# Batch 0's mirrored rows loaded in natural order, their pairs turned and added by TensorE

## The chip, the cores and the metric

The kernel runs on one core of one Trainium2 chip. The metric is the time of one execution on the device in microseconds, as the median of several runs. The profiled execution is one more run, taken with the hardware profiler.

## The reference, cut to what matters

```python
def _attn_ref(x):                      # x: (8, 3136, 256) float32
    X = np.fft.fft(x, axis=1)
    X = np.fft.fft(X, axis=2)
    return X.real.astype(np.float32)

def _moe_ref(x, w_in, conv_w, w_out):  # w_in (256, 1024), conv_w (3, 1024), w_out (1024, 256)
    h = np.maximum(x @ w_in, 0.0)
    # depthwise convolution of width 3 along the sequence, zeros outside
    conv_out = sum(conv_w[k] * shifted(h, k - 1) for k in range(3))
    gate = 1.0 / (1.0 + np.exp(-conv_out))
    return (h * gate @ w_out).astype(np.float32)

out = _moe_ref(_attn_ref(x), w_in, conv_w, w_out)
```

The real part of a two-dimensional Fourier transform, then a gated feed-forward block. The weights come as float64, x as float32.

## The kernel before

The transform of a real input is symmetric, so the kernel works with half of the output rows (NK = S/2 + 1) and with sums and differences of input rows. For each batch it loads x in two halves (`load_ops`), adds to each row its mirror in the sequence and in the feature direction, takes sums and differences further (`fold_ops`), and multiplies the folded tiles with cosine and sine tables (`units`): odd and even output rows, cosine and sine parts, giving two tiles PQ[b]. The second transform and `w_in` are multiplied into one matrix G (`blocks`, `column`), so a step of the main loop does two matmuls (`products`), adds and subtracts them for a row and its mirror with a clamp at zero (`combine`), does the convolution and the gate, and multiplies with `w_out` (`mm2`). One step is one batch, one chunk of the sequence (CUTS) and one of eight blocks of 128 hidden features; loads, folds and units of the next batches are spread over the steps by a table of cycles (`at`, `side`).

All queues are in program order: what is written earlier for an engine runs earlier on it. Tiles come from pools with a fixed number of buffers, and a new tile in a pool waits until the oldest is no longer in use. The change acts in the prologue, before the first step. There:

- `load_ops(0, h)` loads half h of batch 0. A tile `xh` has 8 slots of two rows for each of 98 partitions (99 in the second half, whose last partition holds edge rows). Slots 0 to 3 come by a plain transfer from SP's queue (L119), slots 4 to 7, the mirrored rows, by four indirect transfers from GpSimd's queue (L132) with the index tile `idx`, which lists the partitions backwards.
- `fold_ops(0)` is the list of VectorE steps of both halves: `pair` (L157, L160) adds the mirrored slots to the plain ones, reading features backwards; `both` (L168) adds or subtracts two sums; `evens` (L172, L173); `feats` (L194, L195) folds along the features. `single` and the lines behind it (L179, L200, L202) write the edge columns on GpSimd. `scaled` (L218) turns an operand on ScalarE.
- `mirror_tables` (L319), `mirror_even` (L270) and `mend_row` (L312) complete the tables on ScalarE.
- `taps` turns the convolution weights with an identity on TensorE. `Weight.parts` narrows float64 to float32 (L654 to L677): on VectorE alone, or, where it is given `room`, with one step (L656) on ScalarE.
- `keep_on` issues matmuls of 128 x 128 by 128 x 512 whose result is not used.
- After the folds TensorE runs the four odd units in quarters (`part`), then the feature row (`feature`), `odd_first` (which adds odd entries of the last row to all partitions, from PQ), the even units and `even_first` (the same for even entries, from one row of `e`). Closing sums of the units are on VectorE (L401 to L434, L371 to L385).
- Then come `flip`, `store`, `spread`, the first `seed` and `products` (line L816 and the matmuls to pa and pb), the narrowing of `w_in[1]`, `copies` (L837) and the first `combine` (L845).

The lines of every matmul are those of the helper `mm` (L93), so matmuls are told apart by their tiles.

Of the kernel before, what the change touches and what calls it, by code (L numbers as in the profile page):

```python
# [37 lines left out]
def kernel(  # L38
# [56 lines left out]
    def spare():  # L95
# [8 lines left out]
    nc.gpsimd.iota(idx, pattern=[[0, 1]], base=2 * (NP - 1), channel_multiplier=-2,  # L104
                   allow_small_or_imprecise_dtypes=True)
    sg = const.tile([P, 2, 2], F32, name="sg")
    nc.gpsimd.memset(sg[:, 0], -1.0)
    nc.gpsimd.memset(sg[:, 1], 1.0)

    def load_ops(b, h, eng, other=None, held=False):  # L110


        def plain():
            t = xp.tile([P, 8, 2, D], F32, name="xh", tag="xh")
            xh[b, h] = t
            if held:

                nc.gpsimd.memset(t[0:1, 0, 0, 0:1], 0.0)
# [3 lines left out]

        def zero():
            t = xh[b, h]
            for s0, n, r in ((0, 4, 0), (4, 3, 1), (7, 1, 0)):
                (other or eng).dma_start(out=t[NP:KR, s0:s0 + n], in_=bass.AP(
                    tensor=x.tensor, offset=x.offset + (b * S + r * Q4) * D,
                    ap=[[D, 1], [Q4 * D, n], [0, 2], [1, D]]))
# [11 lines left out]
        return [plain] + [zero] * h + [mirrored(m) for m in range(4)]  # L140

    def fold_ops(b):
# [4 lines left out]
        def half(h):  # L147
# [18 lines left out]
            def both(to, op):  # L166
                def f():
                    vt(flat(to, to + 2), flat(0, 2), flat(2, 4), op=op)  # L168
                return f
# [14 lines left out]
            def feats(odd):  # L184
                def f():
# [12 lines left out]
                    single(odd)()  # L198
                    if odd:
                        gt(w[k, 2:4, qs, P - 1], t()[k, 7:5:-1, :, P], sg[k], op=ALU.mult)  # L200
                    else:
                        nc.gpsimd.tensor_copy(ea[b][k, :, qs], v[:, :, :, P])  # L202
# [28 lines left out]
            ops = [pair(0), pair(2), both(6, ALU.subtract), feats(1), both(4, ALU.add), turned, evens, feats(0)]  # L231
            return ops, {3: single(1), 7: single(0)}, {4: scaled}
# [8 lines left out]
    parted = {}  # L241
# [111 lines left out]
    def units(b):  # L353
# [83 lines left out]
        def feature():  # L437
# [11 lines left out]
            def copy(p):  # L449
                e = hp.tile([P, HW], F32, name="h", tag="h")  # L450
                a_["e"] = [e[:, i * (HO + 2):(i + 1) * (HO + 2)] for i in range(2)]
# [19 lines left out]
        def row():  # L471
            er[b] = erp.tile([1, NK], F32, name="er", tag="er")

        def odd_first(p, n):

            for i in range(2):
                mm(p[:, 1 + 2 * i:n:4], sel[:, i * P:(i + 1) * P], PQ[b][1][:, 1 + 2 * i:n:4], i == 0, True)
# [712 lines left out]
```

## Time and profile before

| | |
|---|---|
| median of 3 runs | 1162.02 us (1161.68 to 1164.53) |
| profiled execution | 1164.47 us, span 1162.7 us |
| mean granted TensorE clock | 0.996 |
| DMA | 167.49 MB, mean 144 GB/s |

A row of the timeline reads: start in us, duration in us, engine, line, operation, tile written <- tiles read, shape, number of instructions merged into the row, and in brackets the idle time of the engine before it with what ended it. PE is TensorE's matmul, PEld its weight load, DVE VectorE, ACT ScalarE, POOL GpSimd, SP the queue of SyncE; a q behind a name is the engine's issuing side. Where rows of one engine overlap, several instructions of other rows ran in between. The granted clock is the share of full speed that TensorE was given.

### The profile page before, as it was taken

How to read it: one execution, taken by the hardware profiler on the slowest of the kernel's cores; microseconds unless marked ns; L12 is line 12 of the kernel's file. 1: busy time of each engine (PE TensorE's matmuls, PEld its weight loads, DVE VectorE, ACT ScalarE, POOL GpSimd, SP SyncE). 2: the span in 40 equal slices, each digit the busy share in tenths (PEclk: the TensorE clock that was granted, in tenths of full speed). 3: DMA queues.
4: the chain of work that ended last, by engine and by line, in shares of the span. 5: the costliest groups of instructions: out<-in, count | busy, mean ns of one | idle time of the engine just before them, and what ended most of it. 6: DMA issues, size and time to landing. Idle time of an engine off the chain costs nothing.

```text
span 1162.7 us, 15082 instructions
## 1 busy us (share of the span) xinstructions
PE 1141.6 (98%) x4834; PEld 893.5 (77%) x4834; DVE 959.8 (83%) x1449; ACT 900.7 (77%) x1702; POOL 379.4 (33%) x493
## 2 busy tenths in 40 slices
PE   6999999999999999999999999999999999999998
PEld 4767777787778777877777877777778787777777
DVE  8699889988987989888878879788886767777775
ACT  3588877877777878887877777887877778888885
POOL 7335523633243152415233332422121221122223
PEclk9899999999999999999999999999999999999999
DMA  9777986786757586757675766865665556666664
GB/s 251 147 122 170 163 153 143 171 174 148 156 121 177 123 186 137 179 108 165 140 175 124 151 139 128 174 130 123 140 125 100 120 118 141 138 129 130 125 116 102
DMA packets 107596, 167.49 MB, mean 144 GB/s; under 512 B 32105, under 2 KB 62839, under 8 KB 107518
## 3 DMA queue, kind: packets, MB, share of 16 engines
q0 software_dynamic: 42160, 115.87, 51.9%
q1 hardware_dynamic: 64616, 50.53, 16.0%
q8 instruction: 38, 0.62, 0.2%
q14 instruction: 41, 0.33, 0.1%
q10 hardware_dynamic: 741, 0.14, 0.1%
HBM read 37.80 MB, written 25.74 MB: 55 GB/s over the span
## 4 chain that ended last, share of the span: by engine, by line
PE 86%; DVE 5%; ACT 4%; POOL 2%; issue 2%; DMA 1%; POOLq 0%; ACTq 0%; DVEq 0%
PE po L93 54%; PE pb L93 13%; PE pa L93 13%; PE pd L93 6%; DVE g L860 1%; DVE g L887 1%; POOL xh L132 1%; ACT os L915 1%; ACT nb L837 1%; DVE h L845 1%; DMA xh<-in_x_dram,idx 1%; ACT g L879 0%; ACT pa L816 0%; ACT g L851 0%; POOL w L179 0%
## 5 line engine op out<-in xcount | busy, mean ns | idle before, releaser
L93 PE MATMUL po<-wout,g 128*128 128x256 f32 x3072 | 706.1, 380 | 3.3 <-DVE g L887 3.3
L93 PEld LDWEIGHTS po<-wout,g 128*128 128x128 f32 x3072 | 581.3, 190 | 147.0 <-issue 17.5
L855 POOL DMA_DIRECT2D g<-h x256 | 219.6, 858 | 729.1 <-ACT g L851 451.4
L837 ACT ACTIVATE nb<-pb 128x386 f32<-128x386 f32 (+3 forms) x512 | 227.6, 499 | 166.4 <-PE pb L93 165.7
L845 DVE CUSTOM_DVE_ANT_0 h<-pa,nb 128x386 f32<-128x386 f32 (+3 forms) x512 | 265.1, 559 | 33.3 <-PE pa L93 22.8
L879 ACT ACTIVATE g<-g,cw 128x770 f32<-128x770 f32 (+3 forms) x264 | 246.1, 935 | 45.5 <-DVE g L860 44.1
L860 DVE SCALAR_TENSOR_TENSOR g<-h,cw,g 128x770 f32<-128x770 f32 (+1 forms) x256 | 265.5, 1037 | 0.0
L887 DVE TENSOR_TENSOR g<-g,h 128x770 f32<-128x770 f32 (+1 forms) x248 | 240.3, 969 | 22.3 <-ACT g L879 22.1
L851 ACT ACTIVATE g<-h,cw 128x770 f32<-128x770 f32 (+1 forms) x256 | 244.2, 954 | 0.0
L93 PE MATMUL pb<-qt,G 127*128 127x387 f32 (+2 forms) x512 | 214.1, 499 | 2.8 <-ACT nb L837 2.4
L93 PE MATMUL pa<-pt,G 128*128 128x387 f32 (+2 forms) x512 | 212.1, 495 | 0.7 <-ACT pa L816 0.7
L816 ACT ACTIVATE pa<-eb,ge 128x387 f32<-128x387 f32 (+2 forms) x256 | 155.4, 607 | 2.0 <-ACT ft L587 0.3
L93 PEld LDWEIGHTS pa<-pt,G 128*128 128x128 f32 x512 | 96.8, 189 | 75.1 <-issue 19.1
L132 POOL DMA_INDIRECT xh<-in_x_dram,idx x64 | 99.5, 1554 | 20.1 <-issue 12.4
L93 PEld LDWEIGHTS pb<-qt,G 127*128 127x128 f32 x512 | 91.3, 191 | 9.8 <-ACT nb L837 4.2
L93 PE MATMUL pd<-tab,w 98*128 98x197 f32 (+2 forms) x448 | 97.7, 317 | 0.0
L93 PEld LDWEIGHTS pd<-tab,w 98*128 98x128 f32 (+1 forms) x448 | 82.1, 191 | 8.8
L915 ACT COPY os<-po 128x256 f32<-128x256 f32 x196 | 57.4, 393 | 6.3 <-PE po L93 6.3
L401 DVE TENSOR_TENSOR as<-as,pd 128x196 f32<-128x196 f32 x14 | 5.0, 358 | 46.1 <-ACT as L397 46.1
L179 POOL COPY w<-xh 98x4 f32<-98x4 f32 (+1 forms) x32 | 38.1, 1190 | 3.7 <-DVE xh L173 2.5
L157 DVE TENSOR_TENSOR xh<-xh 98x1020 f32<-98x1020 f32 (+1 forms) x32 | 38.6, 1210 | 0.5 <-DMA xh<-in_x_dram,idx 0.5
L168 DVE TENSOR_TENSOR xh<-xh 98x1024 f32<-98x1024 f32 (+1 forms) x32 | 38.9, 1215 | 0.1
(150 smaller groups left out, 438.5 us busy)
## 6 DMA issues: line engine op xcount, KB each, us to landing
g<-h POOLq DMA_DIRECT2D x192, 385.0 KB, 4.0
g<-h POOLq DMA_DIRECT2D x64, 416.0 KB, 4.3
out_dram<-os SPq DMA_DIRECT2D x96, 256.0 KB
xh<-in_x_dram SPq DMA_DIRECT2D x16, 784.0 KB
eb<-ed SPq DMA_DIRECT2D x16, 193.5 KB
raw<-in_moe_w_in_dram SPq DMA_DIRECT2D x4, 512.0 KB
raw<-in_moe_w_out_dram SPq DMA_DIRECT2D x1, 2048.0 KB
eb<-ed SPq DMA_DIRECT2D x8, 209.0 KB
```

What stands on the lines that cost most here:

```text
L93: nc.tensor.matmul(o, l, r, start=start, stop=stop, skip_group_check=True)
L132: nc.gpsimd.indirect_dma_start(out=xh[b, h][0:NP, 7 - m].rearrange("p q d -> p (q d)"), out_offset=None, in_=bass.AP(tensor=x.tensor, offs ...
L168: vt(flat(to, to + 2), flat(0, 2), flat(2, 4), op=op)
L816: act(pa[s][:, 0:n], eb[b, c], AF.Copy, scale=ge[:, f:f + 1])
L837: act(nb[s][:, i, cols], p[:, cols], AF.Copy, scale=-1.0 if i else 1.0)
L845: nc.vector._custom_dve(TENSOR_ADD_SAT, out=to, in0=a[:, cols], in1=c[:, i, cols], s0=BIG, s1=0.0)
L851: act(gs[s], hs[s][:, 0:n], AF.Copy, scale=cw[:, 0, s[2]:s[2] + 1])
L855: nc.gpsimd.dma_start(out=gs[s], in_=hs[s][:, 1:1 + n], accum_op=ALU.add)
L860: stt(out=g, in0=h[:, k:k + n], scalar=cw[:, k, f:f + 1], in1=g, op0=ALU.mult, op1=ALU.add)
L879: act(gs[s][:, c], gs[s][:, c], AF.Sigmoid, scale=cw[:, 1, s[2]:s[2] + 1])
L887: vt(g, g, h[:, 0:r.stop], op=ALU.mult)
L915: nc.scalar.copy(out=osb[:, j % 2], in_=pt[:, j % 2])
```

## The change

For batch 0 alone:

- The mirrored rows are no longer gathered backwards. Both transfers of a half are plain: 96 partitions from SP's queue and the last two from GpSimd's (`load_first`). The edge rows come from GpSimd's queue (`edge_rows`).
- A new function `pairs(h)` lets TensorE form the pair sums in PSUM: for each of four slots one product with an identity (128 x 512), one with an identity whose order of partitions is reversed, reading the features backwards (510 columns), and one for column 0 (two columns). ScalarE copies two of the four sums back into `xh`; `both` on VectorE reads the other two from PSUM, in two steps of 512 columns instead of one of 1024. `pair` is left out for batch 0.
- The constants (`con`): identity, reversed identity, and three selecting matrices that ScalarE makes of a tile of ones. `odd_first` and `even_first` use them; `even_first` reads all 128 rows of `e`, which `row` sets to zero first, instead of one row, and is issued after the third of the five remaining units instead of the second.
- The edge columns of the odd tiles are written by ScalarE instead of GpSimd.
- `keep_on` multiplies ones, from the start, and not a weight block; ten products before the pair sums instead of nine before the odd units and two more later; `taps` stands between them.
- `w_in[0]` is narrowed with one step on ScalarE, and the narrowing of `w_in[1]` moves from behind the first `products` to behind the folds and tables, ahead of the odd units.
- The table `dm` is loaded between the two halves of x; `mirror_even` and `mend_row` are issued in another order; `idx` and `half` are made later.

```diff
--- before.py
+++ after.py
@@ -101,31 +101,30 @@
...
     idx = const.tile([P, 1], I32, name="idx")
-    nc.gpsimd.iota(idx, pattern=[[0, 1]], base=2 * (NP - 1), channel_multiplier=-2,
-                   allow_small_or_imprecise_dtypes=True)
-    sg = const.tile([P, 2, 2], F32, name="sg")
-    nc.gpsimd.memset(sg[:, 0], -1.0)
-    nc.gpsimd.memset(sg[:, 1], 1.0)
-    def load_ops(b, h, eng, other=None, held=False):
+    def edge_rows(b, eng):
+        for s0, n, r in ((0, 4, 0), (4, 3, 1), (7, 1, 0)):
+            eng.dma_start(out=xh[b, 1][NP:KR, s0:s0 + n], in_=bass.AP(
+                tensor=x.tensor, offset=x.offset + (b * S + r * Q4) * D,
+                ap=[[D, 1], [Q4 * D, n], [0, 2], [1, D]]))
+    def load_first(h, eng, p0, p1):
+        for s, r in ((0, 1 + 2 * h), (4, Q4 - HO + 2 * (1 - h))):
+            eng.dma_start(out=xh[0, h][p0:p1, s:s + 4], in_=bass.AP(
+                tensor=x.tensor, offset=x.offset + (r + HQ * p0) * D,
+                ap=[[HQ * D, p1 - p0], [Q4 * D, 4], [1, 2 * D]]))
+    def load_ops(b, h, eng):
         def plain():
...
             xh[b, h] = t
-            if held:
-                nc.gpsimd.memset(t[0:1, 0, 0, 0:1], 0.0)
             eng.dma_start(out=t[0:NP, 0:4], in_=bass.AP(
...
                 ap=[[HQ * D, NP], [Q4 * D, 4], [1, 2 * D]]))
-        def zero():
-            t = xh[b, h]
-            for s0, n, r in ((0, 4, 0), (4, 3, 1), (7, 1, 0)):
-                (other or eng).dma_start(out=t[NP:KR, s0:s0 + n], in_=bass.AP(
-                    tensor=x.tensor, offset=x.offset + (b * S + r * Q4) * D,
-                    ap=[[D, 1], [Q4 * D, n], [0, 2], [1, D]]))
         def mirrored(m):
...
@@ -137,7 +136,7 @@
...
             return f
-        return [plain] + [zero] * h + [mirrored(m) for m in range(4)]
+        return [plain] + [lambda: edge_rows(b, eng)] * h + [mirrored(m) for m in range(4)]
     def fold_ops(b):
@@ -165,6 +164,10 @@
...
                 def f():
+                    if b == 0:
+                        for i in range(2):
+                            vt(flat(to + i, to + i + 1), banks[h][i][k], flat(2 + i, 3 + i), op=op)
+                        return
                     vt(flat(to, to + 2), flat(0, 2), flat(2, 4), op=op)
...
@@ -195,10 +198,12 @@
...
                         return
-                    single(odd)()
                     if odd:
-                        gt(w[k, 2:4, qs, P - 1], t()[k, 7:5:-1, :, P], sg[k], op=ALU.mult)
+                        nc.scalar.copy(out=w[k, 0:2, qs, 0], in_=t()[k, s:s + 2, :, 0])
+                        for i, v in ((2, -1.0), (3, 1.0)):
+                            act(w[k, i, qs, P - 1], t()[k, 9 - i, :, P], AF.Copy, scale=v)
                     else:
+                        single(0)()
                         nc.gpsimd.tensor_copy(ea[b][k, :, qs], v[:, :, :, P])
...
@@ -229,6 +234,8 @@
...
             ops = [pair(0), pair(2), both(6, ALU.subtract), feats(1), both(4, ALU.add), turned, evens, feats(0)]
+            if b == 0:
+                return ops[2:], {}, {2: scaled}
             return ops, {3: single(1), 7: single(0)}, {4: scaled}
...
@@ -238,7 +245,7 @@
-    parted = {}
+    parted, banks = {}, {}
     tabs = [const.tile([P, 2, HQ, HE], F32, name="tab2"), const.tile([P, 4, 2, QO], F32, name="tab4")]
...
@@ -447,8 +454,6 @@
...
             def copy(p):
-                e = hp.tile([P, HW], F32, name="h", tag="h")
-                a_["e"] = [e[:, i * (HO + 2):(i + 1) * (HO + 2)] for i in range(2)]
                 for j in range(2):
...
@@ -470,11 +475,15 @@
...
             er[b] = erp.tile([1, NK], F32, name="er", tag="er")
+            e = hp.tile([P, HW], F32, name="h", tag="h")
+            n = HO + 2
+            nc.gpsimd.memset(e[:, 0:2 * n], 0.0)
+            a_["e"] = [e[:, i * n:(i + 1) * n] for i in range(2)]
         def odd_first(p, n):
             for i in range(2):
-                mm(p[:, 1 + 2 * i:n:4], sel[:, i * P:(i + 1) * P], PQ[b][1][:, 1 + 2 * i:n:4], i == 0, True)
+                mm(p[:, 1 + 2 * i:n:4], con[:, (2 + i) * P:(3 + i) * P], PQ[b][1][:, 1 + 2 * i:n:4], i == 0, True)
         def even_first(p, n):
@@ -482,7 +491,7 @@
...
                 for i in range(2):
-                    mm(p[:, 2 * c:n:4], sel[0:1, 2 * P:3 * P], a_["e"][c][0:1, i * o:i * o + m], False, i == 1)
+                    mm(p[:, 2 * c:n:4], con[:, 4 * P:5 * P], a_["e"][c][:, i * o:i * o + m], False, i == 1)
         def flip():
@@ -701,14 +710,10 @@
...
                 f()
-    sel = gp.tile([P, 3 * P], F32, name="sel", tag="g")
-    ident = gp.tile([3 * NF, 3 * NF], F32, name="ident", tag="g")
-    make_identity(nc, ident)
+    con = gp.tile([P, 5 * P], F32, name="con", tag="g")
+    ones = gp.tile([P, 4 * P], F32, name="ones", tag="g")
     cw24 = gp.tile([3 * NF, 1, P], F32, name="cw24", tag="g")
     half = const.tile([P, 1], F32, name="half")
-    nc.gpsimd.iota(half, pattern=[[0, 1]], base=NP - 1, channel_multiplier=-1,
-                   allow_small_or_imprecise_dtypes=True)
-    nc.gpsimd.tensor_scalar(out=half, in0=half, scalar1=0.5, scalar2=0.5, op0=ALU.mult, op1=ALU.add)
     H = F // 2
...
@@ -733,7 +738,7 @@
...
         p = spare()
-        mm(p[:, 0:3 * NF], cw24[:, 0], ident, True, True)
+        mm(p[:, 0:3 * NF], cw24[:, 0], con[0:3 * NF, 0:3 * NF], True, True)
         nc.scalar.copy(out=cw.rearrange("p k m -> p (k m)"), in_=p[:, 0:3 * NF])
...
@@ -744,35 +749,45 @@
...
             vt(cw[:, k], cw[:, k], small, op=ALU.mult)
+    nc.vector.memset(ones, 1.0)
+    w_in[0].load(nc.sync)
+    for h in range(2):
+        xh[0, h] = xp.tile([P, 8, 2, D], F32, name="xh", tag="xh")
+    NB = NP // 16 * 16
+    load_first(0, nc.gpsimd, NB, NP)
+    make_identity(nc, con[:, 0:P])
+    load_first(1, nc.gpsimd, NB, NP)
+    edge_rows(0, nc.gpsimd)
+    load_first(0, nc.sync, 0, NB)
     w_cv.load(nc.scalar)
-    w_in[0].load(nc.sync)
-    for f in load_ops(0, 0, nc.sync):
-        f()
     load_turn(nc.scalar)
-    for f in load_ops(0, 1, nc.sync, None, True):
-        f()
+    nc.sync.dma_start(out=dm, in_=dft_dim[:, :, 0:2])
+    load_first(1, nc.sync, 0, NB)
+    turned_id = con[:, P:2 * P]
+    nc.gpsimd.memset(turned_id, 0.0)
+    nc.gpsimd.affine_select(out=turned_id, in_=turned_id, compare_op=ALU.not_equal, fill=1.0, base=1 - NP,
+                            pattern=[[1, P]], channel_multiplier=1)
+    nc.gpsimd.tensor_copy(con[96:KR, P + NP:P + KR], con[96:KR, NP:KR])
     begin, us, row, flip, store, odd_first, even_first = units(0)
...
     w_cv.narrow(0, 1)
-    w_in[0].narrow(0, 2)
-    taps()
-    act(turn[0:NP, 2], turn[0:NP, 1], AF.Copy, scale=-1.0)
-    nc.gpsimd.memset(dm[0:1, 0, 0, 0:1], 0.0)
+    room = left[:, NF // 2:].rearrange("p f i -> p (f i)").bitcast(I32)
+    for f in w_in[0].parts(0, 2, room):
+        f()
     nc.gpsimd.memset(tabs[1][96:KR, 0:2, 0], 0.0)
-    nc.sync.dma_start(out=dm, in_=dft_dim[:, :, 0:2])
     load_odd(nc.sync, 0)
...
     rest_even(nc.gpsimd)
-    nc.gpsimd.iota(sel[:, 0:P], pattern=[[0, P]], base=1 - P, channel_multiplier=1,
+    nc.gpsimd.iota(half, pattern=[[0, 1]], base=NP - 1, channel_multiplier=-1,
                    allow_small_or_imprecise_dtypes=True)
-    nc.gpsimd.tensor_scalar(out=sel[:, 0:P], in0=sel[:, 0:P], scalar1=0.0, scalar2=1.0, op0=ALU.is_equal, op1=ALU.mult)
-    nc.gpsimd.tensor_scalar(out=sel[:, P:2 * P], in0=sel[:, 0:P], scalar1=-1.0, scalar2=None, op0=ALU.mult)
-    nc.gpsimd.memset(sel[0:1, 2 * P:3 * P], 1.0)
+    nc.gpsimd.tensor_scalar(out=half, in0=half, scalar1=0.5, scalar2=0.5, op0=ALU.mult, op1=ALU.add)
+    nc.gpsimd.iota(idx, pattern=[[0, 1]], base=2 * (NP - 1), channel_multiplier=-2,
+                   allow_small_or_imprecise_dtypes=True)
     for i in (1, 2, 3):
...
@@ -783,7 +798,7 @@
...
         for g in range(2):
-            p = spare()
+            p = spare() if i else psa.tile([P, 512], F32, name="pa", tag="pa")
             for t in range(2):
...
@@ -792,7 +807,7 @@
     def column(i):
-        w, p = w4[i], spare()
+        w, p = w4[i], spare() if i else psb.tile([P, 512], F32, name="pb", tag="pb")
         for m in range(NF // 4):
...
@@ -927,11 +942,33 @@
...
         for _ in range(n):
-            mm(bank, w4[0][:, 0, 0:P], win[0][:, 0].rearrange("p t n -> p (t n)"), True, True)
-    for pool, tag, n in ((psa, "pa", 1), (psa, "pa", 1), (psb, "pb", 7)):
+            mm(bank, ones[:, 0:P], ones, True, True)
+    for pool, tag, n in ((psa, "pa", 1), (psa, "pa", 1), (psb, "pb", 4)):
         bank = pool.tile([P, 512], F32, name=tag, tag=tag)
         keep_on(n)
+    taps()
+    keep_on(4)
+    act(turn[0:NP, 2], turn[0:NP, 1], AF.Copy, scale=-1.0)
+    act(con[:, 2 * P:3 * P], ones[:, 0:P], AF.Copy, scale=con[:, P - 1:P])
+    act(con[:, 3 * P:4 * P], con[:, 2 * P:3 * P], AF.Copy, scale=-1.0)
+    act(con[:, 4 * P:5 * P], ones[:, 0:P], AF.Copy, scale=con[:, 0:1])
+    row()
+    def pairs(h):
+        k = NP if h == 0 else KR
+        t = xh[0, h]
+        banks[h] = [None] * 4
+        for m, (pool, tag) in zip((2, 0, 3, 1), ((psa, "pa"), (psa, "pa"), (psb, "pb"), (psd, "pd"))):
+            p = pool.tile([P, 512], F32, name=tag, tag=tag) if h else spare()
+            banks[h][m] = p
+            v = p.rearrange("p (q d) -> p q d", q=2)
+            mm(p, con[0:k, 0:P], t[0:k, m].rearrange("p q d -> p (q d)"), True, False)
+            mm(v[:, :, 1:D], con[0:k, P:2 * P], t[0:k, 7 - m, ::-1, D - 1:0:-1], False, True)
+            mm(v[:, :, 0], con[0:k, P:2 * P], t[0:k, 7 - m, ::-1, 0], False, True)
+            if m > 1:
+                nc.scalar.copy(out=t[0:k, m].rearrange("p q d -> p (q d)"), in_=p[0:k])
     odds = [us[j] for j in (0, 1, 5, 6)]
...
@@ -943,22 +980,25 @@
...
             ops[j]()
+    pairs(0)
+    blocks(0)
+    column(0)
     folds(0)
+    pairs(1)
     w_out = Weight(wout, moe_w_out.rearrange("(c p) o -> p c o", p=P),
...
     mirror_tables(0)
-    blocks(0)
-    column(0)
-    keep_on(2)
+    mirror_even(0)
     mend_row(1, half)
-    mirror_even(0)
     mirror_tables(1)
+    mirror_even(2)
     folds(1)
-    mirror_even(2)
     mend_row(0, half)
...
     mirror_even(3)
+    for f in w_in[1].parts(0, 2, room):
+        f()
     for f in load_ops(1, 0, nc.sync):
...
@@ -970,24 +1010,21 @@
...
         u.fin()
-    row()
     n = chunks[0].k1
...
             odd_first(p, n)
-        elif i == 1:
+        u.copy()
+        if i == 2:
             even_first(p, n)
-        u.copy()
-        if i == 1:
             eb[0, 0] = ebp.tile([P, HN], F32, name="eb", tag="eb")[:, 0:n]
...
     spread(0, range(1, len(chunks)))
-    room = left[:, NF // 2:].rearrange("p f i -> p (f i)").bitcast(I32)
     steps = [(b, c, f) for b in range(B) for c in range(len(chunks)) for f in range(NF)]
...
@@ -1082,8 +1119,6 @@
...
     seed(steps[1])
-    for f in w_in[1].parts(0, 2, room):
-        f()
     products(steps[0])
...
```

## The prediction

> **What bounds the kernel now.** I read the page first, then the busy time by stretches, then the timeline of the first 50 us, because every line of the change acts before the steady loop starts.
>
> ```profile
> PE 1141.6 (98%) x4834; PEld 893.5 (77%) x4834; DVE 959.8 (83%) x1449; ACT 900.7 (77%) x1702; POOL 379.4 (33%) x493
> 60.00:80.00 20.00, 19.26 (x82) 14.40 (x81) 19.83 (x34) 18.09 (x34) 6.21 (x16) 1.00 0.70 122
> 80.00:100.00 20.00, 18.90 (x76) 13.79 (x75) 19.93 (x30) 17.27 (x41) 6.53 (x8) 1.00 0.68 148
> 47.99 1.02 DVE L845 CUSTOM_DVE_ANT_0 h<-pa,nb 128x385 f32<-128x385 f32 x2
> ```
>
> In the window rows the columns are stretch, length, then PE, PEld, DVE, ACT, POOL busy, granted clock, DMA share, GB/s. TensorE is busy 98% of the span; just behind the start VectorE is full (19.83 and 19.93 of 20 us). The loop's instructions are the same after the change, and neither engine has slack to catch up, so I price everything as a shift of one event: the first `combine` (L845), at 47.99 us now.
>
> How that point comes about:
>
> ```profile
> 11.97 1.22 DVE L157 TENSOR_TENSOR xh<-xh 98x1020 f32<-98x1020 f32 x1 [0.52 <-DMA xh<-in_x_dram,idx]
> 20.99 1.71 ACT L218 ACTIVATE h<-w,turn 98x256 f32<-98x256 f32 x4 [10.30 <-POOL w L200]
> 25.25 0.96 PE L93 MATMUL po<-tab,h 98*128 98x197 f32 x4 [0.78 <-ACT tab L270]
> 27.79 0.68 DVE L195 TENSOR_TENSOR w<-xh 99x508 f32<-99x508 f32 x1
> 33.37 0.88 PE L93 MATMUL pd<-tab,ea 99*1 99x197 f32 x16
> 34.18 0.94 PE L93 MATMUL po<-qt,sel 128*128 128x97 f32 x4
> 34.94 1.05 PE L93 MATMUL po<-tab,w 99*128 99x99 f32 x8
> 35.91 1.13 PE L93 MATMUL po<-h,sel 1*128 1x97 f32 x8
> 36.97 6.96 PE L93 MATMUL po<-tab,w 98*128 98x197 f32 x24
> 44.69 0.89 PE L93 MATMUL pa<-pt,G 128*128 128x386 f32 x2
> 44.93 0.42 DVE L654 TENSOR_SCALAR win<-raw 128x512 int32<-128x512 int32 x1
> 47.04 0.69 DVE L677 SCALAR_TENSOR_TENSOR win<-raw,win 128x512 f32<-128x512 f32 x1
> ```
>
> The mirrored rows hold back a pair sum until 11.97; VectorE folds until 28.47; ScalarE waited 10.30 us for a small GpSimd copy; TensorE starts its real chain at 25.25 and runs it to 43.93. `combine` then waits not for its inputs but for VectorE, which narrows the second weight block from 44.93 to 47.73.
>
> Inside that chain stands a loss:
>
> ```profile
> 36.00:38.00 2.00, 2.00 (x12) 1.91 (x13) 0.63 (x2) 0.81 (x2) 1.64 (x4) 0.85 0.96 207
> 42.00:44.00 2.00, 2.00 (x7) 2.00 (x7) 0.32 (x3) 0.62 (x2) 1.59 (x1) 0.50 0.00 0
> 44.00:46.00 2.00, 1.58 (x4) 0.36 (x3) 1.97 (x5) 0.62 (x1) 0.34 (x3) 0.94 0.01 3
> ```
>
> The granted clock falls to 0.50 at about 37.4 (a mean of 0.85 is 0.6 us of 2 at half) and is back soon after 44, while TensorE runs without a gap. Just before lie thin matmuls: 16 with a one-column weight (33.37), 8 with one row (35.91). The 24 matmuls at 36.97 took 6.96 us. At full clock 8 would go by the 1.05 us row of 34.94 and 16 at 0.21 us each (row at 29.14 below), 4.4 us in all: the drop cost 2.55 us.
>
> **The change, part by part.**
>
> ```profile
> 0.00:5.00 5.00, 0.06 (x1) 0.09 (x1) 3.19 (x8) 0.10 (x1) 3.31 (x15) 1.00 0.53 151
> 5.00:10.00 5.00, 1.21 (x3) 0.91 (x4) 4.43 (x11) 1.46 (x3) 4.17 (x5) 1.00 1.00 281
> xh<-in_x_dram SPq DMA_DIRECT2D x3, 784.0 KB
> raw<-in_moe_w_in_dram SPq DMA_DIRECT2D x4, 512.0 KB
> 4.94 0.59 PE L93 MATMUL po<-ident,cw 24*128 24x24 f32 x2 [4.94 <-DVE cw L677]
> 1.14 1.37 DVE L757 MEMSET qt<- 32x1569 f32 x1 [1.14 <-PEq L1169]
> 9.32 3.78 PE L93 MATMUL pa<-win 128*128 128x512 f32 x4 [3.79 <-DVE win L677]
> 12.89 6.48 PE L93 MATMUL pb<-win 128*128 128x512 f32 x14
> 19.57 1.97 PE L93 MATMUL po<-win,dm 128*128 128x256 f32 x8 [0.20 <-DMA dm<-dft_dim_dram]
> 21.37 0.95 PE L93 MATMUL po<-dm,win 128*128 128x1 f32 x8
> ```
>
> *Transfers.* A block of weights (512 KB) and two of x (784 KB each) are 2.13 MB; the two windows moved 0.76 + 1.40 = 2.16 MB by 10 us. Batch 0's first half should be there at about 10 to 11 us. The eight indirect issues of batch 0 leave GpSimd's queue, seven small direct ones enter it, and nothing waits for that queue before 13 us. On SP the table for dm passes the second half's x, and the tables follow it; at these rates all that is in by 23 us, before its use. SP's load of the output weights waits for a buffer of batch 0's first half until its folds end near 27, batch 1's first load until 38; both are used only in the loop, and no row there waits for them now. The four banks that the first half's pair sums hold come free by then too, ahead of the odd units.
>
> *Warm-up.* The ones need a memset of 512 columns, about 0.45 us by the 1.37 us row for 1569, after 1.14. TensorE starts at 1.7. Ten dummy products are 20 instructions (each float32 product is two). Five cold ones at 3.78/4 = 0.945 us, fifteen at 0.43 (6.48 us less one more cold one, over 13), 0.59 for the taps: pair sums start at 13.3. The x rows are there, so the transfer that held 11.97 is hidden.
>
> *Pair sums on TensorE.* A quarter takes two 512-wide products (four instructions, 0.43 each) and one two columns wide (two instructions, 0.95/8 = 0.12 each): 1.96 us, so 7.85 us per half. No row shows a matmul that reads backwards: the bounds are 0 extra and double for the backward one, +3.4 us per half. I take 0, since reads in steps of two cost nothing visible (1.57 us for 8 in the row at 29.80 below, against 0.83 for 4 without a step). Order on TensorE: pairs 13.3 to 21.15, blocks 1.97 and column 0.95 to 24.1, pairs of the second half to 31.95. Dummies hid beside the folds; these 15.7 us do not: the odd units cannot start at 25.25 any more.
>
> ```profile
> 17.03 0.69 DVE L172 TENSOR_TENSOR xh<-xh 98x512 f32<-98x512 f32 x1
> 17.64 0.69 DVE L173 TENSOR_TENSOR xh<-xh 98x512 f32<-98x512 f32 x1
> 22.60 0.82 ACT L319 ACTIVATE tab<-tab 98x98 f32<-98x98 f32 x4
> 24.02 0.80 ACT L312 ACTIVATE tab<-tab,half 2x196 f32<-2x196 f32 x2
> 24.84 0.62 ACT L270 ACTIVATE tab<-tab 99x196 f32<-99x196 f32 x2
> 28.33 1.13 ACT L312 ACTIVATE tab<-tab,half 2x393 f32<-2x393 f32 x2
> 29.14 0.83 PE L93 MATMUL po<-tab,w 99*128 99x196 f32 x4
> 29.80 1.57 PE L93 MATMUL po<-tab,h 98*128 98x197 f32 x8
> 31.77 0.36 DVE L427 TENSOR_TENSOR as<-as,po 128x196 f32<-128x196 f32 x1 [0.28 <-ACT as L421]
> 32.43 0.57 DVE L432 TENSOR_TENSOR qt<-as 128x392 f32<-128x392 f32 x1
> 37.08 0.48 ACT L985 COPY eb<-po 128x386 f32<-128x386 f32 x1 [0.35 <-PE po L93]
> ```
>
> *VectorE* loses the two 1.22 us sums of each half. After the last pair bank it has nine steps of 512 columns left; such rows last 0.69 us but start 0.61 apart (17.03, 17.64). One half-sum and two for the odd features end at 33.9, the other six at 37.6, where the folds ended at 28.47 before. Behind them now stands the narrowing of the second weight block, moved from 44.93. The move takes its 2.8 us out of the way of `combine`, but puts them ahead of the units' closing sums.
>
> *ScalarE.* New are two copies per half out of PSUM (0.6 each, by 0.48 for 386 columns) and three edge writes (0.2 each) that GpSimd did; the 10.30 us wait goes. But its queue is in order, and the table mirrors stand behind the copies of the second half: third quarter ready 30.0, copied 30.6, mirrors and mends 0.82 + 0.62 + 0.80 + 0.82 + 0.62 to 34.25, edges 34.85, the turned operands (1.71) to 36.55. Then come another mend (1.13), two more mirrors (2 x 0.62) and ScalarE's 0.7 us share of the narrowing: 39.6. VectorE's last two steps of it wait for that and end at 41.0.
>
> *Odd units.* On TensorE the first two parts took 3.7 us from 25.25: now 31.95 to 35.65. The last parts need the turned operands: 0.83 to 36.5, 1.57 from 36.65, then 0.83 and 1.57 to 40.6, feature row 0.88 to 41.5. Next in line is `odd_first`, which reads the odd unit's sums. VectorE gets to them at 41.0: 2 x 0.36, then 0.66 (31.77 to 32.43) and 2 x 0.57, so 43.5. TensorE stands 2.0 us, with all the closing work queued behind it.
>
> *End.* `odd_first` 0.7, even-even 1.05, even 1.7, `even_first` 1.13, 1.05, 1.7: 7.3 us, to 50.8. The closing sum 0.57, product 0.89 and hops of 0.1: `combine` at 52.5, which is **+4.5 us**.
>
> *Clock.* `even_first` gets full rows, and moves behind a full unit; by that alone the drop would go. But the feature row and the 2.0 us stall put 2.9 us with almost no work in the same place. Before, the 3.4 us up to the drop at about 37.4 held 0.7 us of `odd_first`, 1.05 of even-even and 0.4 of a full unit beside thin ones, and it dropped. I expect the same: **+2.55 us**, as work of the same length follows. A rule stands against this: the Trainium skill, "TensorE: Matmul & The Clock Gate", Part 1, has the clock fall only after about 3.4 us of idleness. The trace differs: the clock fell with TensorE busy throughout. By that rule the 2.0 us gap would be harmless, and the sum would stop at the +4.5.
>
> Sum: +7.05 us. The profiled execution is 1164.47 us (span 1162.7), so it would become 1171.5; it lies 2.45 above the median 1162.02, against which I forecast **1169.1 us**.
>
> **The rivals.**
>
> *The clock holds.* For it: the full-row edge sum and the skill's rule; against it: the rows with 0.50. 1162.0 + 4.5 = 1166.5.
>
> *No stall.* If VectorE reaches the odd sums before TensorE needs them (the narrowing fits into its waits for the pair banks and mirrors), the 2.0 us and the drop both go: 1162.0 + 2.5 = 1164.5. Against it: VectorE and TensorE both count from the same last pair bank, so an early start helps neither against the other.
>
> *Faster.* The pair sums cost less than I read: if a product with an identity needed one instruction instead of two, a quarter is 1.0 us, the second half ends 7.7 us sooner, and at best all of that passes on: 1166.5 - 7.7 = 1158.8. It decides below 1.96 - 4.5/8 = 1.40 us a quarter. Against it: every float32 product in the trace is two instructions.
>
> *Slow backward product.* At double, TensorE loses 6.9 us more: 1166.5 + 6.9 = 1173.4 without the drop. The Trainium skill, "Advanced Engine Details and Errata", Memory Cachelines, says patterns that are not contiguous slow matmuls in PSUM; the new output has runs of 255. The trace gives it weak support: stepped outputs of 97 columns took 0.235 us each (34.18), those of 99 in smaller steps 0.131.
>
> **How the numbers follow.** Forecast 0.40; clock holds 0.25; no stall 0.15; faster 0.10; slow backward product 0.10. About 0.3% (3.5 us) is what a measurement can tell from no change: 1158.5 to 1165.5. Faster 0.10; same 0.20 (no stall, and 0.05 of the clock-holds case, whose start may be 1 us early); slower 0.70. The range leaves out the faster case and the upper part of the slow one: 1163 to 1174.
>
> **What would show it.** Right: the second half's pair sums end near 32 us; quarters of about 1.96 us; `odd_first` waits for VectorE about 2 us; granted clock 0.50 for some 7 us after it; first L845 near 55. Wrong: quarters under 1.4 us or over 2.6; x rows landing after 13.3; dummies on ones that do not raise the clock, so that pair sums run at 0.85 us an instruction; or a loop that absorbs the shift between 50 and 140 us.

## The result, and the profile after

| | before | after |
|---|---|---|
| median | 1162.02 us (5 runs, 1161.59 to 1164.53) | 1170.12 us (5 runs, 1169.14 to 1172.75) |
| profiled execution, span | 1164.47 us, 1162.7 us | 1170.12 us, 1168.3 us |
| mean granted clock of the profiled execution | 0.996 | 0.997 |

The change makes the kernel slower by 8.1 us in the median, a ratio of 1.0069 with a 95% interval of 1.0049 to 1.0089. The two profiled executions lie only 5.65 us apart, and the reason matters for everything below: executions of before come with and without the fall of the granted clock near 37 us. Of 25 executions that ran beside the first four experiments, 18 had a mean clock of 0.999 or more and 1161.5 to 1163.2 us (median 1161.76); 7 had 0.996 or 0.997 and 1164.3 to 1164.9 us. The profile of before is one of the second kind; by its time, the median run is one of the first.

The page's busy shares after:

```profile
PE 1155.1 (99%) x4880; PEld 901.1 (77%) x4880; DVE 954.5 (82%) x1446; ACT 905.3 (77%) x1716; POOL 372.0 (32%) x484
```

TensorE has 46 more instructions and 13.5 us more busy time, of which part fills time in which it stood before (its first instruction came at 4.94 us, now at 1.47); the span grew by 5.6 us. The timeline of after, with the rows that answer to those of before:

```profile
1.47 3.63 PE L93 MATMUL pa<-ones 128*128 128x512 f32 x4 [1.47 <-DVE ones L752]
12.33 1.02 PE L93 MATMUL po<-xh,con 98*128 98x512 f32 x2
13.58 7.02 PE L93 MATMUL po<-xh,con 98*128 98x510 f32 x22 [0.23 <-DMA xh<-in_x_dram]
23.08 4.01 PE L93 MATMUL pa<-xh,con 99*128 99x512 f32 x12
28.89 2.08 PE L93 MATMUL pd<-xh,con 99*128 99x512 f32 x6
30.83 0.58 PE L93 MATMUL po<-tab,w 98*128 98x196 f32 x2
31.06 0.69 DVE L169 TENSOR_TENSOR xh<-pa,xh 99x512 f32<-99x512 f32 x1 [3.90 <-ACT tab L277]
31.24 0.86 PE L93 MATMUL po<-tab,h 98*128 98x197 f32 x4
37.89 0.72 ACT L665 ACTIVATE win<-win,low 128x512 int32<-128x512 int32 x1
39.26 0.88 PE L93 MATMUL pd<-tab,ea 99*1 99x197 f32 x16
39.56 0.69 DVE L686 SCALAR_TENSOR_TENSOR win<-raw,win 128x512 f32<-128x512 f32 x1
41.36 0.57 DVE L439 TENSOR_TENSOR qt<-as 128x392 f32<-128x392 f32 x1
42.07 0.95 PE L93 MATMUL po<-qt,con 128*128 128x97 f32 x4 [1.94 <-DVE qt L439]
42.84 4.57 PE L93 MATMUL po<-tab,w 99*128 99x99 f32 x16
51.35 0.81 PE L93 MATMUL pb<-qt,G 127*128 127x386 f32 x2
52.26 0.89 PE L93 MATMUL pa<-pt,G 128*128 128x386 f32 x2
53.33 1.03 DVE L860 CUSTOM_DVE_ANT_0 h<-pa,nb 128x385 f32<-128x385 f32 x2 [0.40 <-PE pa L93]
60.55 1.02 DVE L860 CUSTOM_DVE_ANT_0 h<-pa,nb 128x385 f32<-128x385 f32 x2 [1.48 <-POOL h L837]
63.43 1.03 DVE L860 CUSTOM_DVE_ANT_0 h<-pa,nb 128x385 f32<-128x385 f32 x2 [0.19 <-POOL h L837]
```

The odd units start at 30.83, and the row that answers to the one at 25.25 of before is at 31.24, 6.0 us later. VectorE is still narrowing the second weight block until 40.25 (39.56 + 0.69), so its closing sum of the odd unit comes at 41.36, and `odd_first` (42.07) has waited 1.94 us for it. The first `combine` (now L860) is at 53.33, 5.34 us later than before. By stretches, with the granted clock third from the right:

```profile
40.00:42.00 2.00, 0.13 (x4) 0.00 (x0) 1.97 (x7) 0.32 (x1) 1.52 (x2) 1.00 0.89 304
42.00:44.00 2.00, 1.93 (x10) 1.96 (x11) 1.97 (x6) 1.45 (x5) 1.70 (x2) 0.59 1.04 236
46.00:48.00 2.00, 2.00 (x9) 2.00 (x8) 0.56 (x2) 0.00 (x0) 0.57 (x2) 0.50 0.82 76
48.00:50.00 2.00, 2.00 (x14) 2.00 (x14) 0.49 (x2) 0.48 (x1) 0.47 (x1) 0.70 0.15 26
```

A mean of 0.59 is 1.64 us at half in the second row, and 0.70 is 1.2 us in the last: the clock fell at 42.36 and was back at 49.20. In 40 to 42 VectorE is full and TensorE empty. The third and fourth `combine` of before, not shown there, give the shift that stays:

```profile
54.32 1.02 DVE L845 CUSTOM_DVE_ANT_0 h<-pa,nb 128x385 f32<-128x385 f32 x2 [0.57 <-POOL h L822]
57.21 1.02 DVE L845 CUSTOM_DVE_ANT_0 h<-pa,nb 128x385 f32<-128x385 f32 x2 [0.20 <-PE pa L93]
```

Both come 6.2 us later in after (60.55 and 63.43), and at the end of the two executions the difference is 5.65: the loop gave about half a microsecond back.

### The profile page after: what moved, and what is told of

It reads as the page before. It is cut to its first block, busy times and chain, and to the rows that moved or that the text cites. A ratio compares the mean times of both kernels' runs of the same rounds, so it can differ in the third digit from the quotient of the medians.

```text
span 1168.3 us, 15194 instructions
## 1 busy us (share of the span) xinstructions
PE 1155.1 (99%) x4880; PEld 901.1 (77%) x4880; DVE 954.5 (82%) x1446; ACT 905.3 (77%) x1716; POOL 372.0 (32%) x484
## 4 chain that ended last, share of the span: by engine, by line
PE 86%; DVE 5%; ACT 4%; DMA 2%; issue 2%; POOL 0%; SPq 0%; ACTq 0%; DVEq 0%
PE po L93 54%; PE pb L93 13%; PE pa L93 13%; PE pd L93 6%; DMA xh<-in_x_dram 2%; DVE g L875 1%; ACT os L930 1%; ACT nb L852 1%; DVE g L902 1%; DVE h L860 1%; ACT g L894 0%; DMA raw<-in_moe_w_in_dram 0%; ACT pa L831 0%; POOL w L182 0%; ACT g L866 0%
## 5 line engine op out<-in xcount | busy, mean ns | idle before, releaser
L860 DVE CUSTOM_DVE_ANT_0 h<-pa,nb 128x386 f32<-128x386 f32 (+3 forms) x512 | 265.7, 561 | 32.6 <-PE pa L93 23.0
L131 POOL DMA_INDIRECT xh<-in_x_dram,idx x56 | 89.4, 1597 | 17.5 <-issue 11.0
L171 DVE TENSOR_TENSOR xh<-xh 98x1024 f32<-98x1024 f32 (+1 forms) x28 | 34.1, 1216 | 0.0
L156 DVE TENSOR_TENSOR xh<-xh 98x1020 f32<-98x1020 f32 (+1 forms) x28 | 33.9, 1211 | 0.0
```

What stands on the lines that cost most here:

```text
L131: nc.gpsimd.indirect_dma_start(out=xh[b, h][0:NP, 7 - m].rearrange("p q d -> p (q d)"), out_offset=None, in_=bass.AP(tensor=x.tensor, offs ...
L860: nc.vector._custom_dve(TENSOR_ADD_SAT, out=to, in0=a[:, cols], in1=c[:, i, cols], s0=BIG, s1=0.0)
```

## The experiments

Theory after this result: three parts make the loss. The pair sums stand in series on TensorE in front of the odd units; the early narrowing makes `odd_first` wait; and the wait lets the clock fall. Each experiment takes one of them away or puts a part of the change into before. Its ratio is taken against runs of before on the same chip; the runs of after are not from the same batch as those of the experiments.

**e1: after, with the narrowing of the second block back behind the seeds.**

```diff
     mirror_even(3)
-    for f in w_in[1].parts(0, 2, room):
-        f()
...
     seed(steps[1])
+    for f in w_in[1].parts(0, 2, room):
+        f()
     products(steps[0])
```

> The changed kernel with one part undone: the second weight block is narrowed behind the first products again. Theory (the narrowing ahead of the closing sums makes TensorE stand at odd_first, and the stand drops the clock): odd_first waits under 0.5 us instead of 1.94, the granted clock stays at 1.00 from 40 to 50 us, the first pa product comes at about 48 us instead of 52.26, time about 1166 us. Rival A (the feature row's thin matmuls drop the clock by themselves): the wait goes, the clock still falls to 0.50, time about 1168.3. Rival B (ScalarE's queue or a transfer sets the closing sums): nothing moves, 1170.

Measured: 1166.66 us (8 runs, 1165.90 to 1167.52), ratio 1.0030 (1.0019 to 1.0041), mean clock 0.999 or more in every run. Its timeline, then its stretches:

```profile
40.30 0.94 PE L93 MATMUL po<-qt,con 128*128 128x97 f32 x4
47.47 0.89 PE L93 MATMUL pa<-pt,G 128*128 128x386 f32 x2
51.45 1.02 DVE L860 CUSTOM_DVE_ANT_0 h<-pa,nb 128x385 f32<-128x385 f32 x2
60.26 1.02 DVE L860 CUSTOM_DVE_ANT_0 h<-pa,nb 128x385 f32<-128x385 f32 x2 [0.19 <-POOL h L837]
```

```profile
42.00:44.00 2.00, 2.00 (x15) 2.00 (x15) 1.12 (x4) 0.63 (x2) 1.67 (x3) 1.00 1.05 204
```

`odd_first` has no wait, the clock holds, and 3.5 us of the loss are gone in the medians (3.16 between the profiled executions). What remains, 4.9 us over the undisturbed 1161.76, belongs to the rest of the change. The first product to pa comes 4.79 us sooner than in after, the first `combine` only 1.88: it waits for the narrowing again. The time fell by more than the `combine` moved, so the first `combine` alone isn't the event that sets the loop. The fourth does better: it comes 3.17 us sooner than in after, and the profiled execution is 3.16 us shorter.

**e2: after, with two products on ones in the place of the stall.**

```diff
         if i == 0:
+            bank = psb.tile([P, 512], F32, name="pb", tag="pb")
+            keep_on(2)
             p = spare()
             odd_first(p, n)
```

> The changed kernel with two dummy products (four instructions of 128x512, about 1.7 us) between the feature row and odd_first, where TensorE stands for 1.9 us. Theory (the stand starves the clock's activity measure): odd_first starts as late as before, at about 42.1 us, but the granted clock stays at 1.00 and the closing units run at full speed, 2.5 us saved, about 1167.6 us. Rival (the Trainium skill, TensorE: Matmul & The Clock Gate, Part 1: only some 3.4 us of idleness count, so a 1.9 us gap is not the cause): the clock falls all the same, 1170 us.

Measured: 1167.39 us (5 runs, 1166.95 to 1167.73), ratio 1.0036 (1.0022 to 1.0050), mean clock 0.999 or more throughout. Timeline, then stretches:

```profile
39.98 1.98 PE L93 MATMUL pb<-ones 128*128 128x512 f32 x4
41.98 0.91 PE L93 MATMUL po<-qt,con 128*128 128x97 f32 x4
42.71 2.47 PE L93 MATMUL po<-tab,w 99*128 99x99 f32 x16
48.21 0.81 PE L93 MATMUL pb<-qt,G 127*128 127x386 f32 x2
```

```profile
42.00:44.00 2.00, 2.00 (x15) 2.00 (x16) 1.97 (x7) 1.52 (x6) 1.67 (x3) 1.00 1.01 239
```

`odd_first` starts at 41.98, as late as in after (42.07), but TensorE was busy until then and the clock stays at 1.00: the 16 matmuls behind it take 2.47 us instead of 4.57, and the first product to pb comes at 48.21 instead of 51.35. This shows that the idle 1.94 us, and not the lateness, brought the clock down. The drop is worth 2.7 us of time (1170.12 - 1167.39; the two did not run side by side). Against e1 the early narrowing costs another 0.7 us by the medians and nothing by the profiled executions (1166.97 and 1166.96), so with the stall filled its price isn't told apart from zero.

**e3: before, with `even_first` on 128 rows.** The tile of `e` and the selecting matrix are set to zero ahead, on GpSimd behind the first half's folds, and the product reads all rows, as after does.

```diff
...
-                    mm(p[:, 2 * c:n:4], sel[0:1, 2 * P:3 * P], a_["e"][c][0:1, i * o:i * o + m], False, i == 1)
+                    mm(p[:, 2 * c:n:4], sel[:, 2 * P:3 * P], a_["e"][c][:, i * o:i * o + m], False, i == 1)
```

> The kernel before with one part of the change: even_first reads 128 rows of e (127 of them zero) with a 128-row selecting matrix instead of one row; place and number of matmuls stay. Theory (matmuls over one row count as idleness for the clock): the clock stays at 1.00 from 36 to 46 us, the 24 matmuls behind it take about 4.4 us instead of 6.96, time about 1159.5 us. Rival (the one-column weights of the feature row, or the narrow outputs, drop it): the clock falls as before, 1162 us.

Measured: 1161.58 us (11 runs, 1161.42 to 1161.92), ratio 0.9991 (0.9982 to 0.9999). Timeline, then stretches:

```profile
35.77 1.33 PE L93 MATMUL po<-h,sel 128*128 128x97 f32 x8
36.93 3.89 PE L93 MATMUL po<-tab,w 98*128 98x197 f32 x24
```

```profile
38.00:40.00 2.00, 2.00 (x17) 2.00 (x16) 1.25 (x3) 0.57 (x2) 0.36 (x1) 1.00 0.99 184
```

The 24 matmuls behind the edge sum take 3.89 us instead of 6.96, and none of the 11 runs has the drop. The median hardly moves, since most runs of before had no drop to lose: this is where it came out that the profile of before isn't like its median. So the expected 1159.5 us did not come, though the clock held as the theory had it. The gain is in the spread: 0.5 us wide here, 3.3 us for before.

**e4: before, with the narrowing early and the thin rows kept.** 
```diff
     mirror_even(3)
+    for f in w_in[1].parts(0, 2, room):
+        f()
...
     seed(steps[1])
-    for f in w_in[1].parts(0, 2, room):
-        f()
     products(steps[0])
```

> The kernel before with one other part of the change: the second weight block is narrowed behind the folds, ahead of the odd units. Theory (a cost without a gain: the first combine is freed by 0.9 us, but the steps behind it are set by products and copies): the odd units' closing sums come 1 to 2 us later, odd_first waits about as long, 1163 to 1164 us. Rival (the first combine sets the loop): about 1161 us.

Measured: 1163.65 us (12 runs, 1160.39 to 1165.06), ratio 1.0003 (0.9991 to 1.0014): two groups again. Five runs without a drop have a median of 1160.90, seven with a mean clock of 0.996 or 0.997 lie between 1163.60 and 1165.06. The profiled execution is of the first group:

```profile
34.45 0.91 PE L93 MATMUL po<-qt,sel 128*128 128x97 f32 x4 [0.30 <-DVE qt L432]
37.21 3.96 PE L93 MATMUL po<-tab,w 98*128 98x197 f32 x24
44.89 1.02 DVE L845 CUSTOM_DVE_ANT_0 h<-pa,nb 128x385 f32<-128x385 f32 x2 [2.30 <-POOL h L822]
```

The median lies within the expected 1163 to 1164 us by luck: it is that of the runs with the drop, and the expectation had the wrong sign for the narrowing. In before, VectorE's folds end at 28.47 and it has a gap to narrow in; `odd_first` waits only 0.30, and without a drop the move gains about 0.9 us. In after no such gap is left. But the drop came in 7 of 12 runs, against 7 of 25 for before beside it: a short wait in front of thin matmuls seems to make it more frequent, on few runs.

**e5: before, with the edits of e3 and e4 together**, that is

```diff
...
-                    mm(p[:, 2 * c:n:4], sel[0:1, 2 * P:3 * P], a_["e"][c][0:1, i * o:i * o + m], False, i == 1)
+                    mm(p[:, 2 * c:n:4], sel[:, 2 * P:3 * P], a_["e"][c][:, i * o:i * o + m], False, i == 1)
...
     mirror_even(3)
+    for f in w_in[1].parts(0, 2, room):
+        f()
```

> The kernel before with the two parts that helped there: full rows in even_first and the second weight block narrowed behind the folds. Theory (the two act on different things: the rows keep the clock up in every run, the early narrowing takes 1.0 us out of the way of the loop's first steps where VectorE has a wait to fill): 1160.6 us with a spread under 1 us, faster than both kernels. Rival (the early narrowing delays odd_first and the clock falls in half of the runs as it did with the thin rows): about 1163 us.

Measured: 1160.64 us (12 runs, 1159.96 to 1161.86), ratio 0.9982 (0.9973 to 0.9990), no drop in any run, and faster than before and after. The first `combine` then waits for a GpSimd step:

```profile
45.54 1.02 DVE L845 CUSTOM_DVE_ANT_0 h<-pa,nb 128x385 f32<-128x385 f32 x2 [3.29 <-POOL h L822]
```

So two parts of the change are good in themselves, 1.1 us together against the undisturbed runs of before beside it (1161.71); what loses is the rest.

**e6: e1, with the turned products of the second half left out.** The mirrored rows of that half are then missing from the output.

```diff
-            mm(v[:, :, 1:D], con[0:k, P:2 * P], t[0:k, 7 - m, ::-1, D - 1:0:-1], False, True)
-            mm(v[:, :, 0], con[0:k, P:2 * P], t[0:k, 7 - m, ::-1, 0], False, True)
+            if h == 0:
+                mm(v[:, :, 1:D], con[0:k, P:2 * P], t[0:k, 7 - m, ::-1, D - 1:0:-1], False, True)
+                mm(v[:, :, 0], con[0:k, P:2 * P], t[0:k, 7 - m, ::-1, 0], False, True)
```

> The changed kernel with the narrowing put back, and the turned products of the second half left out (eight wide and eight two-column instructions, about 4.1 us of TensorE; the mirrored rows of batch 0's second half are then missing from the output). Theory (TensorE's own time for the pair sums sets the start of the odd units): the odd units start about 4 us earlier, at 27 us instead of 31, and the time falls by 3 to 4 us, to about 1163 us. Rival (VectorE's folds, ScalarE's queue or the arrival of x set it): under 1 us, 1166 us.

Measured: 1163.84 us (10 runs, 1163.02 to 1164.42), ratio 1.0004 (0.9994 to 1.0014).

```profile
26.14 0.50 PE L93 MATMUL po<-tab,w 98*128 98x196 f32 x2
43.21 0.89 PE L93 MATMUL pa<-pt,G 128*128 128x386 f32 x2
48.48 1.02 DVE L860 CUSTOM_DVE_ANT_0 h<-pa,nb 128x385 f32<-128x385 f32 x2 [1.88 <-POOL h L837]
56.74 1.02 DVE L860 CUSTOM_DVE_ANT_0 h<-pa,nb 128x385 f32<-128x385 f32 x2
```

The odd units start at 26.14 and the first product to pa comes 4.26 us sooner than in e1. The time falls by 2.8 us in the median, on another chip than e1's (3.57 between the profiled executions; the fourth `combine` comes 3.52 us sooner). Sixteen instructions of the pair sums are thus worth about 3 us, and the rival of e6 (under 1 us) falls: the series on TensorE makes more than half of the 4.9 us that e1 left, with the first half's sums and the plain products not yet counted.

**e7: e1, without the four products on ones behind `taps`.** The rivals were that these dummies set when the pair sums start, or that the arrival of x does.

```diff
     taps()
-    keep_on(4)
     act(turn[0:NP, 2], turn[0:NP, 1], AF.Copy, scale=-1.0)
```

> The changed kernel with the narrowing put back and without the four dummy products ahead of the pair sums (3.4 us of TensorE). Theory (the x rows arrive at 12.3 and 13.5 us and set the start of the pair sums, the dummies only fill the wait): the pair sums start no more than 0.5 us earlier, and the time is that of the kernel with the dummies, 1166.7 us, if the clock holds. TensorE then stands some 3 us: if so short a stand drops the clock, as the stand at odd_first seemed to, the pair sums run at 0.85 us an instruction and some runs are 2 to 4 us longer; by the Trainium skill (TensorE: Matmul & The Clock Gate, Part 1: about 3.4 us of idleness) none are. Rival (the dummies set the start): 3 us faster, 1163.5 us.

Measured: 1173.21 us (6 runs, 1168.92 to 1174.29), ratio 1.0088 (1.0073 to 1.0103), mean clock 0.993 to 0.996. Timeline, then stretches:

```profile
9.42 1.10 PE L93 MATMUL po<-xh,con 98*128 98x512 f32 x2 [0.35 <-DMA xh<-in_x_dram]
13.06 9.90 PE L93 MATMUL po<-xh,con 98*128 98x510 f32 x22 [2.55 <-DMA xh<-in_x_dram]
```

```profile
10.00:12.00 2.00, 0.51 (x2) 0.00 (x0) 0.81 (x6) 0.00 (x0) 1.13 (x2) 1.00 1.13 203
12.00:14.00 2.00, 0.94 (x1) 0.50 (x2) 0.00 (x0) 0.00 (x0) 1.24 (x5) 0.51 1.12 245
18.00:20.00 2.00, 2.00 (x7) 1.01 (x6) 0.00 (x0) 0.00 (x0) 0.00 (x0) 0.78 1.01 205
```

The first product starts 2.9 us sooner, and the next waits for the mirrored rows until 13.06, where after has it at 13.58 and e1, from which e7 differs by the dummies alone, at 13.81: the transfer sets the start to within three quarters of a microsecond. The wait lets the clock fall at 12.04 (0.51 is 1.96 of 2 us at half), about 1.5 us after TensorE last worked, and the 22 instructions take 9.90 us instead of 7.02. The dummies hold the clock and cost at most those three quarters. The profile shown is the fastest of the six runs, 1168.92 us at a mean clock of 0.996; the other five have 0.993 or 0.994 and lie between 1172.81 and 1174.29. They lost more clock than this one fall, and no trace shows where.

**e8: e5, with the zeroing step of the first loop step issued ahead of `flip`.** The aim was the GpSimd step that e5's `combine` waits for.

```diff
...
+    row_of(steps[0])
     flip()
     store()
...
-    row_of(steps[0])
     seed(steps[0])
```

> The kernel before with full rows and early narrowing, and besides the zeroing of the first step's edge columns on GpSimd put ahead of the sign change of the edge row, which waits for a transfer. Theory (with the clock held and the narrowing out of the way, the first combine waits 3.29 us for that zeroing, and the third step's copies then follow it): the first combine comes at about 42.8 us instead of 45.54, some 1 to 2 us of it reach the end, about 1159.3 us. Rival (the loop's first steps are set by ScalarE's copies and TensorE's blocks, so the first combine is not what counts): 1160.6 us.

Measured: 1160.13 us (12 runs, 1159.74 to 1161.33), ratio 0.9980 (0.9971 to 0.9989), the fastest version here.

```profile
42.83 1.02 DVE L845 CUSTOM_DVE_ANT_0 h<-pa,nb 128x385 f32<-128x385 f32 x2 [0.40 <-PE pa L93]
43.04 1.99 POOL L491 TENSOR_SCALAR er<-er 1x392 f32<-1x392 f32 x1 [4.05 <-DMA er<-qt]
```

In GpSimd's queue the zeroing stood behind a step that waits for a transfer (4.05 us here); ahead of it, the first `combine` comes 2.71 us sooner. Only 0.5 us reaches the end, less than the expected 1 to 2. Again an early first `combine` isn't an early loop: the fourth moved by 0.86 us (53.79 to 52.93), and the profiled execution by 0.76.

**e9: e6 with the edit of e8.**

```diff
+    row_of(steps[0])
     flip()
     store()
```

> The changed kernel with the narrowing put back and the turned products of the second half left out (mirrored rows of that half missing from the output), and the zeroing put ahead in the same way. Without it the products were 4.3 us earlier than with all pair sums, but the time fell by 2.8 us only, and the first combine waited 1.88 us for the zeroing. Theory (that wait swallowed the rest): about 1162.4 us. Rival (the rest was lost elsewhere): 1163.8 us.

Measured: 1163.61 us (10 runs, 1162.69 to 1164.13), ratio 1.0011 (1.0002 to 1.0020). The first `combine` comes 1.87 us sooner than in e6, the median moves by 0.2 us:

```profile
46.61 1.02 DVE L860 CUSTOM_DVE_ANT_0 h<-pa,nb 128x385 f32<-128x385 f32 x2
55.84 1.03 DVE L860 CUSTOM_DVE_ANT_0 h<-pa,nb 128x385 f32<-128x385 f32 x2 [0.19 <-PE pa L93]
```

By the medians the wait for GpSimd isn't what kept e6 from its full 4.26 us. The profiled executions say otherwise: the fourth `combine` comes 4.42 us sooner than in e1 and the execution is 4.27 us shorter (1162.69 against 1166.96), against 3.57 in e6. The runs of each version spread over some 1.4 us and e1 ran on another chip, so this isn't settled.

## Why the prediction was right or wrong, point by point

The account by medians, from a before without the drop at 1161.76 us: the change without the early narrowing 4.9 us (e1), the early narrowing with its stall filled 0.7 (e2 against e1, not told apart from zero), the fall of the clock 2.7 (after against e2). The three are differences of medians that follow each other, so they add up to 1170.1 by construction.

- **The forecast lay 1.0 us below the median, but that is luck: two errors cancelled in it.** The step that failed is the base, "it lies 2.45 above the median 1162.02, against which I forecast". The 2.45 us are the clock's drop in the profiled execution of before; the sum had credited the change with ending that drop (the +4.5 counts from a `combine` at 47.99 that had paid it; in e3, without the drop, it comes at 45.56) and then charged a new one. Most runs have nothing to be credited with, so against the median 2.45 us more were due. The other way, the sum was too long by 1.4 us: 7.05 forecast, 5.65 between the profiled executions. 7.05 - 1.4 + 2.45 is the 8.1 us measured.
- **Start of the pair sums: 13.3 forecast, 12.33 measured**; the first dummy came 0.2 us sooner than forecast (1.47 against 1.7), and the dummies took less (the forecast's own terms add up to 13.5, not 13.3). The x rows were later than "10 to 11 us": the second product waited for them until 13.58, in e7 until 13.06. That is behind the 13.3 that the prediction named as a sign of being wrong; it cost only 0.23 us, since the dummies covered the rest.
- **Quarter: 1.96 us forecast.** The last quarter runs from 28.89 to the odd units' first matmul at 30.83, 1.94 us. The second half's pairs end there too (forecast 31.95), early by what the start was early. The rivals *faster* and *slow backward product* both fall here: the products that read backwards cost what a plain one costs. The rule under Memory Cachelines in the Trainium skill, "Advanced Engine Details and Errata", does not show in this pattern of runs of 255.
- **VectorE and the stall: right in size, by another path.** Narrowing forecast to end at 41.0, measured 40.25; stall 2.0 against 1.94; `odd_first` 43.5 against 42.07, of which the start explains 1.0. The forecast let VectorE wait for ScalarE's share of the narrowing until 39.6. That share was done at 38.61 (37.89 + 0.72), and from 31.06 to the closing sums VectorE had no idle row. It had ten steps of folds behind the last pair bank and not nine: by the code, the first half-sum writes a slot that the last quarter's product still reads. The rival *no stall* falls, as the stall is there; e1 shows what its absence is worth: 3.5 us, clock and all.
- **Closing work: 7.3 us forecast, 6.2 us at full clock** (e2, 41.98 to 48.21). This term and the start were 2.5 us too long together; a larger drop (0.5), a longer way from the last unit to the `combine` (0.3) and 0.3 us more behind it took back 1.1 of it.
- **The clock: right that it falls, and after the stall; 2.55 forecast, 2.7 us in time.** On TensorE it was worth 3.05 us (`odd_first` to the first product to pb takes 9.28 us in after and 6.23 in e2). The 2.55 came from an estimate of 4.4 us for the 24 matmuls of before at full clock; e3 shows 3.89, so there, too, the drop cost 3.07. The rival *clock holds* falls, for the median run at least (one of the five has a mean clock of 0.999, and 1169.20 us). In the Trainium skill, "TensorE: Matmul & The Clock Gate", Part 1, a full window of about 3.4 us of idleness goes ahead of a fall. The trace differs: 1.94 us of standing behind a 0.88 us row of one-column matmuls was enough, and e2 shows that work in just that gap prevents it. What exactly is counted as activity isn't shown.
- **The event that the sum was made for.** The first `combine` was taken as the point that sets the loop. It moved by 5.34 us and the time by 5.65; but e8 and e9 have it 2.7 and 1.9 us sooner than e5 and e6 and gain 0.5 and 0.2. The better event is the fourth `combine`. Over the eleven profiled executions the time from the first one to the end of the span differs by 2.45 us, from 1113.1 to 1115.6. From the fourth it is 1105.4 to 1105.5 in the five kernels built from before and 1104.8 to 1105.1 in the six built from after. In after the fourth moved by 6.2, so the sum held in part because the first `combine` moved with it. Why the kernels built from after take some half a microsecond less behind that point isn't shown.
- **Not foreseen:** ScalarE waited 5.86 us for a transfer before the selecting matrices, until 14.94, so the first copy out of PSUM came at 15.97. Nothing waited for it.

Still open: why the runs of after with a mean clock of 0.998 or 0.999 (1169.14 and 1169.20) are 1.8 us above e2; where the two runs of 1172.60 and 1172.75, with 0.994 and 0.993, lost still more clock; and whether half of the turned products gave their full 4.26 us. The natural-order loads alone, without the pair sums on TensorE, weren't tried.

## What to carry to other kernels

Before a sum is set against a median, see whether the profiled execution is like the median one: the mean clock of each run told it here. Before a shift in a prologue is priced by one event, see from which event on all versions take the same time; here it was the fourth `combine`, not the first. An engine that only runs dummies is free until real work is put in series on it; price that work from the stage that it delays, and try good parts of a change alone (full rows and the early narrowing, without the rest, won 1.1 us). Where TensorE had to wait some two microseconds beside thin matmuls, products on ones in the gap cost less than the fall of the clock here (e2). Where the thin matmuls alone lay ahead of the fall, zero rows that made one product full were enough (e3).

## What the hardware showed that was not expected

The three falls of the clock in these traces lasted the same time, by the window means: 6.84 us in before (37.40 to 44.24), in after (42.36 to 49.20) and in e7 (12.04 to 18.88), though TensorE had work again at most 1.0 us after the fall (13.06 in e7). The amounts of idleness ahead of them differed: none before (thin matmuls only), 1.94 us in after, about 1.5 us in e7. And it differs from run to run of one program: of the 70 runs of before beside the experiments, 20 have a mean clock below 0.999 (7 of 25, 8 of 23, 5 of 22); with the edge sum filled up to 128 rows it held in all 11 (e3), and with the early narrowing as well in all 12 of e5 and all 12 of e8.
